# Attention with a sliding window, then a token-mixing MLP: queries kept in even and odd halves from the transposes to the output store

## The chip, the cores and the metric

One Trainium2 chip, one core of it. The metric is the device time of one execution in microseconds (us). Engines: TensorE (PE), VectorE (DVE), ScalarE (ACT), GpSimd (POOL) and SyncE (SP); here POOL issues all loads and SP all stores.

## What is computed

Eight batches, eight heads, 576 tokens, 64 features a head. Attention with a causal window of 128 tokens and a linear penalty on the distance, then an MLP that mixes tokens with weights made from the tokens themselves:

```python
scores = scale * np.matmul(q, k.transpose(0, 1, 3, 2))
rel = pos[:, None] - pos[None, :]
bias = slopes[:, None, None] * (-np.abs(rel).astype(np.float32))[None, :, :]
mask = (rel >= 0) & (rel < window)            # window = 128
scores = np.where(mask, scores + bias[None], -1000000000.0)
attn = softmax(scores)
x = np.matmul(attn, v)                        # heads side by side: (8, 576, 512)

wq, wk = x @ w_q, x @ w_k                     # (8, 576, 64) each
W_tok = scale * np.einsum('bsd,btd->bst', wq, wk)
mixed = np.einsum('bst,btd->bsd', W_tok, x)
out = np.maximum(mixed, 0.0) @ w_out          # (8, 576, 512), float32
```

## The kernel before

All work inside is fp16 with fp32 in PSUM. For each batch the kernel goes through these steps; the names in parentheses are the operations of its plan, with their lines.

- **Loads** (POOL, L239). Tokens 0 to 511 of q and k come in two chunks of 256 tokens into `nat`. In batches 1 to 5 a partition holds two neighbouring tokens of each head ("two-token rows": one transfer of 256 KB a chunk). In batches 6 and 7 (`ONE`) it holds one token ("one-token rows": two transfers of 128 KB a chunk). The last 64 tokens go to `ntl`, q below and k above. Batch 0 has a form of its own, six tokens a partition, in a part of the output buffer that is free at that time.
- **Transposes** (PE, L339 for batch 0, L366 for two-token rows, L360 for one-token rows, L382 for the tail) into a PSUM bank, 1024 columns a chunk, where tokens of even number stand ahead of those of odd number if the rows were two-token rows. An **eviction** (L220 on ACT, L222 on DVE, helper `cp`) copies the bank into `qkT`, which has the features on partitions and the tokens along the row, and puts even and odd tokens in turn as it does so.
- **Scores** (PE, L415): for each pair of heads and each half of the sequence, 64 keys at a time against their window of up to 192 queries, so that keys stand on the PSUM partitions and queries along the row. ACT takes the exponential (L420); DVE multiplies by the table of penalties `bt`, which is also the mask (L435, L439).
- **Values** (PE, L459) with a column of ones for the sum, DVE divides (L472, L475) into `x`, which has 128 tokens on partitions; PE transposes x (L491) and a copy puts it into `xT`.
- **Mixing** (PE, L508, L526, L538, L554; relu on ACT L561 or DVE L563), for two batches at a time up to the output: 1152 tokens in 9 tiles of 128. A tile is four matmuls (L575), a copy from PSUM into one of 14 output buffers `osa` (L220 on ACT or L222 on DVE), and a **store** by SP (L582) of 128 tokens x 512 float32, 256 KB. There are 36 tiles and 36 stores.

What runs when is fixed by a table, `ORDER`: every operation of the plan stands in it once, by its number, with a letter for its engine (A, D, G, S, P for ACT, DVE, POOL, SP, PE) and, for PE, its PSUM bank. Each engine works through its own operations in that order; between engines, semaphores guard data and buffers. A later tile that takes an output buffer again waits until the store of the earlier tile has landed. SP goes through its stores in the order of the table, which begins with tiles 12, 5, 3, 1, 13, 2, 0, 11.

At the start POOL writes the difference of column and row into `rel` (iota, L245), DVE makes the identity for the transposes from it (`idn`), and the table `bt` from the same numbers.

Of the kernel before, what the change touches and what calls it, by code (L numbers as in the profile page):

```python
# [13 lines left out]
P = 128  # L14
S = 576
# [16 lines left out]
175P5+1/4 141G 68D 20A 69D 89P0 176A 140G 24D 70P4 90D 152A 100P2 91D 227G 101D 188P0 102D 92P5 229G 189A  # L32
103P7 71A 230G 190D 155P0+1/2 93D 177P2 104D 231G 178A 191D 105P4+1/4 232G 156A 179D 240P7 416G 106A 180D
# [3 lines left out]
332P5 284A 339D 270P0 174A 233G 250P2 333D 251A 197P6 271A 234G 281P2 252D 330P5 198A 253D 414G 199A 200P4  # L37
272P0 201D 282A 327G 331D 259P6 336P4 273A 334P3 202P2 337A 610G 274D 203D 261P0+1/0 260A 335D 285D 353P2 262A
325G 340P4 275D 342P6 341A 129P1 286D 328G 354A 206P4 431P0 263D 329G 130A 264D 210P2 207A 418G 211A 287P4
326G 343A 254P2 288D 432A 289D 276P6 415G 425P1 255D 256D 290P0 419G 426A 204P4 277D 291D 265P2 602G 278D 205A  # L40
351P0 266D 352A 417G 257P5 344D 126P4 267D 506G 373P0 355D 127A 279P7 258D 507G 268P6 280D 123P5 269A 356D
424G 364P2 292P6 124D 365A 420G 345D 374A 362P4 423G 429P3 293D 363A 375P0 706G 294D 295P2 376A 427P5 510G
296A 430D 208P0 346P6 428A 377D 511G 366D 433P4 347D 209A 348D 435P2 297P5 434A 508G 457P0 298D 436A 303P4
458A 601G 304D 446P2+1/6 459P6 367D 357P0 460A 422G 448P4 447A 358D 461D 517P7 509G 359D 470P2 421G 378D 301P0
212P6 302A 518D 604G 449A 305P0 306A 608G 521P5+1/4 471A 437P0 349P7 603G 438A 523P4 350D 368P2 705G 213D 524A
379P0 701G 369D 450D 522A 468P6 380D 519P4 370D 609G 469A 525P5 439D 520A 605G 381D 371P7 120P6 526A 606G 472D
451D 382P4 527P0 614G 372A 299P2 440D 360P5 528A 221P7 607G 383D 361A 538P0 300D 697G 222A 384P4 121D 539A
704G 462D 616P7 385A 452P0 698G 617A 386D 560P2 215P6 516G 561A 453D 454D 562P4 514G 387P7 563A 473D 441P2
703G 620P1 216A 564D 529P4 618P0 611G 530A 565D 224P6 388A 512G 531D 540P4 619D 515G 307P7 541A 442D 716P0
513G 225A 542D 463P4 621A 443D 389P6 612G 308A 464D 622P1 717A 465D 613G 390A 551P2 623D 549P4 395P6 699G  # L50
712P0 550A 532D 624P1 396A 702G 713D 391P4 552A 474P6 625D 700G 392A 637P2 475D 626P0 476D 710G 720P5 627A
218P4 721D 638A 709G 628P0 543D 393P6 615G 397P2 629A 310P5 394A 708G 630D 533P0 219D 311A 650P6 711G 398A
534D 477P4 535D 444P5 651A 648P2 707G 553D 639P0 649A 445D 313P7 631D 640A 714P6 314D 718P5 715A 455P3 478D
566P0 554D 719A 316P2 567D 568D 735P4 317A 733P6 456D 632P0 736A 318S 641D 217S 131S 125S 724P2 734A 633D
555P4 634D 722P6 725A 556D 544P0 557D 723A 744P2 545D 399P5 546D 745A 659P6 726D 400A 746P0 642D 661P2 466P4
401S 662A 128S 122S 405P5 315S 223S 467D 660A 652D 643P2 747A 663D 479P6 644D 664D 406A 411P4 407S 480A 226S
312S 645D 558P5 481A 727D 569P1 482P0 412A 536P3 547P2 483D 559A 728P6 548D 537A 484P0 748D 570D 755P4 729D
485A 757P2 730D 408P1 756A 653D 758A 571P6 409A 749D 490P2 410S 665P0 309S 572A 214S 220S 413S 491D 646P5 573A
574P4 666D 654P2 667D 647A 635P7 575A 655D 488P0 492P5 656D 576P4 489A 636D 493A 657P3 737D 668P2 577A 486P0
658D 578P4 584P6 759D 503P3 579A 585D 487A 750P4 760D 669A 582P0 580P6 738D 402P2 583A 581A 751D 761P0 752D  # L60
504A 739P6 762D 763D 670P4 740D 731P3 741D 764P1 732A 753P0 765D 742P7 497P6 671D 743A 586P3 754A 403A 766P0
587D 589P7 588S 767A 673P3 672A 494P2 590D 768A 674D 769P5 592P7 498A 770D 499S 675P6 404S 591S 593A 771P3
495A 676D 496S 679P0 681P4 594S 772D 505S 683P6 595P2 680A 684D 682A 773P0 677P6 596A 775P4 598P3 678D 597S
776D 694P2 599A 691P7 695D 685P6 774D 696S 692D 500P5 686A 693S 777P0 687S 600S 779P2 501A 784P7 778D 502S
780D 688P6 785D 793P5 689D 786S 787P4 690S 794D 790P7 795S 788A 781P6 789S 791D 792S 782A 783S
"""
# [84 lines left out]

ONE = (6, 7)
PTW = 64 + 4 * 256
# [5 lines left out]
def kernel(  # L159
# [81 lines left out]
    def setup():  # L241
        plan.op("zero", ("DVE",), lambda e: nc.vector.memset(wz, 0.0), writes=["wz"])  # L242
        plan.op("one", ("DVE",), lambda e: nc.vector.memset(wone, 1.0), writes=["wone"])
        plan.op("iota", ("POOL",),
                lambda e: nc.gpsimd.iota(rel, pattern=[[1, 256]], base=0, channel_multiplier=-1),  # L245
                writes=["rel"])
        plan.op("idn", ("DVE",),
                lambda e: nc.vector.tensor_scalar(out=idn, in0=rel[:, 0:128], scalar1=0, scalar2=None,
                                                  op0=ALU.is_equal), reads=["rel"], writes=["idn"])
# [43 lines left out]
    def load_qk(b):  # L293
        if b == 0:
            for h in range(0, H, 2):
                for x, src in ((0, q), (1, k)):
                    load("ldsix", six[x][:, h : h + 2, :], src[b, h : h + 2].rearrange("h (p j) d -> p h (j d)", j=6),
                         [("six", x, h // 2)])
            return
        n = b % NN  # L300
        for c in range(2):
            for x, src in ((0, q), (1, k)):
                if b in ONE:
                    for j in range(2):
# [24 lines left out]
    def transposes(b):  # L329
        T = qkT[b % NQ]  # L330
        if b == 0:
            for hp in range(4):
                for x in range(2):
# [7 lines left out]

                    def ev(e, hp=hp, x=x, g=g):
                        cp(e, T[:, x, hp, :].rearrange("t (p j) -> t p j", j=6),
                           ps16(g)[:, 0:S].rearrange("t (j p) -> t p j", j=6))
# [5 lines left out]
        for z in range(2):  # L350
            for x in range(2):
                g = Ps(1)

                def tr(e, z=z, x=x, g=g):
                    o = ps16(g).rearrange("t (y j p) -> t y j p", y=4, j=2)
                    if b in ONE:
# [20 lines left out]
            if z == 0:  # L377
# [17 lines left out]
    def attention(b):  # L395
        for hp in range(4):
# [3 lines left out]
            for u in range(2):  # L400
                g = Ps(2)

                def sc(e, u=u, hp=hp, g=g):
# [7 lines left out]
                    for half, c, w, k0, q0 in mms:  # L411
                        for a in range(2):
                            r = slice(64 * a, 64 * a + 64)
                            o = 512 * a + c
                            nc.tensor.matmul(ps32(g)[half : half + 64, o : o + w],  # L415
                                             T[r, 1, hp, k0 : k0 + 64], T[r, 0, hp, q0 : q0 + w],
                                             start=True, stop=True)
# [81 lines left out]
    def mixing(b):  # L499
# [68 lines left out]
        for o in range(0, 512, 128) if i == 0 else range(512, 2 * S, 128):  # L568
# [12 lines left out]
            def st(e, o=o, n=n):  # L581
                nc.sync.dma_start(out=out[2 * p : 2 * p + 2].rearrange("b t c -> (b t) c")[o : o + 128, :], in_=osb[n])  # L582

# [54 lines left out]
```

## Time and profile before

| | |
|---|---|
| time, 3 runs | 150.2 us median (149.82 to 150.21) |
| profiled execution | 150.23 us, span 148.1 us |
| mean granted TensorE clock | 0.997 |
| loads (POOL's queue) | 14.82 MB in 85648 packets |
| stores (SP's queue) | 9.44 MB in 5184 packets, 36 transfers |
| first and last store issued | 101.9 and 144.9 us |

The span runs from the first instruction to the last; the profiled execution's own time is 2.1 us longer. In the rows, a group gives the line, the engine, the operation, output and input by the program's names, and "x" the number of instructions; three numbers with strokes are the shortest, the median and the longest duration in ns. The windows view gives, for a stretch of the span, the busy time of each engine. "A <- B" in the waits means that A waited and B released it. The DMA share in slices and windows is that of the 16 DMA engines; above 1 it counts packets that overlap.

### The profile page before, as it was taken

To read this page: it belongs to the slowest core of one execution; us is meant where nothing else is said; L and a number is where in the kernel's file an instruction comes from. 1 tells how busy PE (TensorE), PEld (TensorE's weight loads), DVE (VectorE), ACT (ScalarE), POOL (GpSimd) and SP (SyncE) were. 2 spreads that over 40 slices of the span, in tenths; PEclk is the share of its full clock that TensorE was granted. 3 is DMA by queue.
4 is the path that set the end of the run, shared out by engine and by line. 5 is a ranking of instruction groups with operands and counts; after the bars stand their busy time and mean duration, and the time that the engine had idled before them with its cause. 6 is when DMAs were issued, how large, how long until landed. Compare 5 with 4: busy or idle time off the path is not lost.

```text
span 148.1 us, 5381 instructions
## 1 busy us (share of the span) xinstructions
PE 136.3 (92%) x2314; PEld 88.3 (60%) x2314; DVE 119.0 (80%) x223; ACT 115.5 (78%) x181; POOL 85.6 (58%) x111
## 2 busy tenths in 40 slices
PE   6999889898799889999999999999999999999990
PEld 2345546676576476566576657576686858554430
DVE  1763799898979979988699989899989999367760
ACT  6428998789889988797999988998998984774311
POOL 6998999998565899599989996920000000000000
PEclk9999999999999999999999999999999999999998
DMA  2999999999999999999999999992586710158794
GB/s 20 147 145 163 169 162 123 157 177 175 181 174 182 168 146 148 180 156 149 157 156 156 151 136 148 106 134 93 222 302 252 293 61 4 71 189 304 265 341 180
DMA packets 90855, 24.59 MB, mean 166 GB/s; under 512 B 84176, under 2 KB 86224, under 8 KB 90832
## 3 DMA queue, kind: packets, MB, share of 16 engines
q0 software_dynamic: 85648, 14.82, 128.8%
q1 hardware_dynamic: 5184, 9.44, 17.1%
q8 instruction: 18, 0.29, 0.8%
q14 instruction: 5, 0.04, 0.1%
HBM read 29.62 MB, written 9.44 MB: 264 GB/s over the span
## 4 chain that ended last, share of the span: by engine, by line
PE 63%; ACT 17%; DVE 10%; issue 4%; POOL 2%; DMA 1%; DVEq 0%; POOLq 0%; ACTq 0%
PE psb L575 19%; PE psb L459 9%; ACT pt L420 8%; PE psb L415 7%; PE psb L491 6%; PE psb L508 5%; ACT qkT L220 4%; PE psb L554 4%; PE psb L366 3%; PE psb L360 3%; PE psb L538 3%; DVE x L475 2%; ACT rm L561 2%; PE psb L592 2%; PE psb L339 2%
## 5 line engine op out<-in xcount | busy, mean ns | idle before, releaser
L420 ACT ACTIVATE pt<-psb 128x768 f16<-128x768 f32 x64 | 49.8, 822 | 5.0 <-PE psb L415 3.5
L239 POOL DMA_DIRECT2D vn<-in_v_dram x44 | 36.7, 861 | 4.9 <-DMA natq<-in_q_dram 1.7
L575 PE MATMUL psb<-wout,rm 128*128 128x512 f16 x144 | 35.4, 380 | 0.3 <-ACT pt L420 0.3
L439 DVE TENSOR_TENSOR pt<-pt,bt 128x1536 f16<-128x1536 f16 x32 | 29.9, 950 | 0.2
L475 DVE TENSOR_TENSOR x<-psb,inv 128x640 f16<-128x640 f32 x32 | 26.1, 818 | 0.8
L220 ACT COPY qkT<-psb 128x1024 f16<-128x1024 f16 (+2 forms) x26 | 22.7, 891 | 4.3 <-PE psb L339 3.4
L415 PE MATMUL psb<-qkT 64*64 64x192 f16 (+2 forms) x640 | 21.1, 235 | 2.7 <-ACT qkT L220 1.3
L459 PE MATMUL psb<-vn,pt 128*128 128x65 f16 x576 | 22.3, 193 | 1.0 <-DVE pt L439 0.5
L459 PEld LDWEIGHTS <-pt 128*128 128x128 f16 x576 | 20.1, 98 | 4.0 <-DVE pt L439 0.7
L575 PEld LDWEIGHTS <-rm 128*128 128x128 f16 x144 | 12.6, 98 | 13.6 <-issue 1.7
L220 ACT COPY osa<-psb 128x512 f32<-128x512 f32 x23 | 13.6, 594 | 8.9 <-PE psb L575 7.7
L415 PEld LDWEIGHTS <-qkT 64*64 64x64 f16 x640 | 11.9, 106 | 12.5 <-issue 7.9
L222 DVE COPY qkT<-psb 128x1024 f16<-128x1024 f16 (+2 forms) x17 | 14.4, 856 | 5.2 <-PE psb L339 3.9
L239 POOL DMA_DIRECT2D natq<-in_q_dram x18 | 16.7, 936 | 0.7 <-DMA natk<-in_k_dram 0.4
L239 POOL DMA_DIRECT2D natk<-in_k_dram x18 | 16.8, 952 | 0.0
L435 DVE TENSOR_TENSOR pt<-pt,bt 128x512 f16<-128x512 f16 x32 | 13.2, 414 | 3.5 <-ACT pt L420 3.4
L592 PE MATMUL psb<-wz 128*128 128x512 f16 x38 | 14.2, 469 | 1.6 <-DVE wz L242 1.3
L561 ACT ACTIVATE rm<-psb 128x576 f16<-128x576 f32 x20 | 12.5, 663 | 2.3 <-PE psb L554 2.0
L491 PE MATMUL psb<-idn,x 128*128 128x128 f16 x160 | 12.7, 220 | 0.4 <-DVE x L475 0.2
L222 DVE COPY osa<-psb 128x512 f32<-128x512 f32 x13 | 8.8, 686 | 4.2 <-PE psb L575 2.9
L220 ACT COPY xT<-psb 128x576 f16<-128x576 f16 x15 | 9.4, 648 | 3.1 <-PE psb L491 3.1
L491 PEld LDWEIGHTS <-x 128*128 128x128 f16 x160 | 9.5, 98 | 2.6 <-DVE x L475 0.6
(63 smaller groups left out, 163.4 us busy)
## 6 DMA issues: line engine op xcount, KB each, us to landing
out_dram<-osa SPq DMA_DIRECT2D x36, 256.0 KB, 2.6
vn<-in_v_dram POOLq DMA_DIRECT2D x28, 128.0 KB, 5.2
natk<-in_k_dram POOLq DMA_DIRECT2D x10, 256.0 KB, 6.9
natq<-in_q_dram POOLq DMA_DIRECT2D x10, 256.0 KB, 6.8
vn<-in_v_dram POOLq DMA_DIRECT2D x16, 64.0 KB, 4.8
natq<-in_q_dram POOLq DMA_DIRECT2D x8, 128.0 KB, 5.3
natk<-in_k_dram POOLq DMA_DIRECT2D x8, 128.0 KB, 5.3
osa<-in_k_dram POOLq DMA_DIRECT2D x4, 144.0 KB, 4.6
```

Source lines behind the costliest of these rows:

```text
L220: nc.scalar.copy(o, i)
L222: nc.vector.tensor_copy(out=o, in_=i)
L239: plan.op(name, ("POOL",), lambda e: nc.gpsimd.dma_start(out=dst, in_=src), reads=reads, writes=writes)
L415: nc.tensor.matmul(ps32(g)[half : half + 64, o : o + w], T[r, 1, hp, k0 : k0 + 64], T[r, 0, hp, q0 : q0 + w], start=True, stop=True)
L420: nc.scalar.activation(out=blocks(pt)[:, :, 2 * u : 2 * u + 2, 0:192], in_=ps32(g).rearrange("t (a c) -> t a c", a=2)[:, :, 0:384].rearran ...
L439: nc.vector.tensor_tensor(out=o, in0=o, in1=bt[:, 2 * hp : 2 * hp + 2, 0:192].unsqueeze(2).broadcast_to([P, 2, 4, 192]), op=ALU.mult)
L459: nc.tensor.matmul(ps32(g)[:, o : o + D + 1], pt[:, a, c : c + 128], vv[:, kb, 2 * hp + a, 0 : D + 1], **flags)
L475: nc.vector.tensor_tensor(out=xb[:, :, 128 * hp : 128 * hp + 128].rearrange("t j (a d) -> t a j d", a=2), in0=px()[:, :, :, 0:D], in1=iv.u ...
L491: nc.tensor.transpose(ps16(g)[:, 128 * t : 128 * t + 128], xb[:, t, 128 * hp : 128 * hp + 128], idn)
L561: nc.scalar.activation(out=o, in_=s, func=AF.Relu, scale=WSCALE)
L575: nc.tensor.matmul(ps32(g), rm[p % NR][:, db, o : o + 128], wout[:, db, :], start=(db == 0), stop=(db == 3))
L592: nc.tensor.matmul(psb[:, b, :], wz[:, 0:P], wz[:, 0:DM], start=True, stop=True)
```

## The change

Queries are no longer put into the order of the tokens. For q, `qkT` now holds all even tokens and then all odd ones, as the transposes leave them in PSUM. From there on each strip of 64 queries (scores, weights, x, mixed tokens, output tile) has its 32 even tokens first and then its 32 odd ones; keys and values stay in order.

- The eviction of q copies 1024 columns as they lie (for batch 0, even and odd are parted on the way); that of the tail becomes two copies, one for q that parts even and odd, one for k.
- The moving operand of the scores takes, for each strip, 32 columns from the even half and 32 from the odd half.
- iota and the identity are written in the permuted order, so that penalties and transposes match.
- `ONE` holds batches 4 to 7, but for k alone: k of batches 4 and 5 now comes in one-token rows, q of batches 6 and 7 in two-token rows. The table is the same order with new numbers; where a load became two they stand side by side or near, where two became one the later is gone.
- A store of 128 tokens becomes two of 64 buffer rows, each with the even tokens and then the odd ones to their places in DRAM.

```diff
-ONE = (6, 7)
+ONE = (4, 5, 6, 7)
...
-                lambda e: nc.gpsimd.iota(rel, pattern=[[1, 256]], base=0, channel_multiplier=-1),
+                lambda e: nc.gpsimd.iota(rel, pattern=[[64, 4], [1, 2], [2, 32]], base=0, channel_multiplier=-1),
...
-                lambda e: nc.vector.tensor_scalar(out=idn, in0=rel[:, 0:128], scalar1=0, scalar2=None,
+                lambda e: nc.vector.tensor_scalar(out=idn.rearrange("t (s m j) -> t s m j", s=2, j=2),
+                                                  in0=rel[:, 0:128].rearrange("t (s j m) -> t s m j", s=2, j=2),
+                                                  scalar1=0, scalar2=None,
...
-                if b in ONE:
+                if x == 1 and b in ONE:
...
+                        if x == 0:
+                            cp(e, T[:, x, hp, :].rearrange("t (j p i) -> t j p i", j=2, i=3),
+                               ps16(g)[:, 0:S].rearrange("t (i j p) -> t j p i", i=3, j=2))
+                            return
                         cp(e, T[:, x, hp, :].rearrange("t (p j) -> t p j", j=6),
...
+                    if x == 0:
+                        cp(e, T[:, x].rearrange("t y (j p) -> t y j p", j=2)[:, :, :, P * z : P * z + P],
+                           ps16(g).rearrange("t (y j p) -> t y j p", y=4, j=2))
+                        return
...
-                    cp(e, T[:, :, :, 512:576], ps16(g)[:, 0:512].rearrange("t (y x c) -> t x y c", y=4, x=2))
+                    s = ps16(g)[:, 0:512].rearrange("t (y x c) -> t x y c", y=4, x=2)
+                    cp(e, T[:, 0].rearrange("t y (j p) -> t y j p", j=2)[:, :, :, 256:288],
+                       s[:, 0].rearrange("t y (p j) -> t y j p", j=2))
+                    cp(e, T[:, 1, :, 512:576], s[:, 1])
...
-                            nc.tensor.matmul(ps32(g)[half : half + 64, o : o + w],
-                                             T[r, 1, hp, k0 : k0 + 64], T[r, 0, hp, q0 : q0 + w],
+                            n = w // 64
+                            d = ps32(g)[half : half + 64, o : o + w].rearrange("t (s j m) -> t s j m", s=n, j=2)
+                            s = T[r, 0, hp, :].rearrange("t (j s m) -> t s j m", j=2, m=32)
+                            nc.tensor.matmul(d, T[r, 1, hp, k0 : k0 + 64], s[:, q0 // 64 : q0 // 64 + n],
...
-                nc.sync.dma_start(out=out[2 * p : 2 * p + 2].rearrange("b t c -> (b t) c")[o : o + 128, :], in_=osb[n])
+                d = out[2 * p : 2 * p + 2].rearrange("b t c -> (b t) c")
+                for z in range(2):
+                    nc.sync.dma_start(out=d[o + 64 * z : o + 64 * z + 64, :].rearrange("(m j) c -> j m c", j=2),
+                                      in_=osb[n][64 * z : 64 * z + 64])
```

The start of SP's list of stores, each with the semaphores that it waits for (DMAHW0 to 7 are eight counters that the transfers of SP take in turn, and each transfer waits for the one that last had its counter; DMASW are those of the loads). Before:

```order
L582 DMA out_0_dram<-osa_112 128x512 [waits DMASW0_49,Activation_49]
L582 DMA out_0_dram<-osa_112 128x512 x2
L582 DMA out_0_dram<-osa_112 128x512 [waits DVE_49]
L582 DMA out_0_dram<-osa_112 128x512 [waits DMASW5_49,Activation_49]
L582 DMA out_0_dram<-osa_112 128x512
```

In the changed kernel:

```order
L601 DMA out_0_dram<-osa_112 2x32x512 [waits DMASW0_49,Activation_49]
L601 DMA out_0_dram<-osa_112 2x32x512 x5
L601 DMA out_0_dram<-osa_112 2x32x512 [waits DVE_49]
L601 DMA out_0_dram<-osa_112 2x32x512
L601 DMA out_0_dram<-osa_112 2x32x512 [waits DMAHW0_49,DMASW5_49,Activation_49]
L601 DMA out_0_dram<-osa_112 2x32x512 [waits DMAHW1_49]
```

Each store stands there twice, its DRAM side has even/odd as its first dimension, and the first wait for a counter of SP's own comes with the fifth tile instead of the ninth.

On ACT, the evictions of batch 1 (`qkT1`) between the exponentials of batch 0 (`pt`), before:

```order
L220 COPY qkT1_83<-psb_113 128x4x256
L420 ACTIVATE pt3_89<-psb_113 128x2x2x192
L220 COPY qkT1_83<-psb_113 128x4x256
L420 ACTIVATE pt2_88<-psb_113 128x2x2x192
L220 COPY qkT1_83<-psb_113 128x8x64
```

And in the changed kernel:

```order
L222 COPY qkT1_83<-psb_113 128x4x256
L437 ACTIVATE pt3_89<-psb_113 128x2x2x192
L222 COPY qkT1_83<-psb_113 128x8x128
L437 ACTIVATE pt2_88<-psb_113 128x2x2x192
L222 COPY qkT1_83<-psb_113 128x8x32
L222 COPY qkT1_83<-psb_113 128x4x64
```

Nothing moved there; q's copy (the second) has another shape, and the tail's copy has become two.

More of the change, by code (lines that the diff above doesn't have):

```diff
@@ L32 @@
 175P5+1/4 141G 68D 20A 69D 89P0 176A 140G 24D 70P4 90D 152A 100P2 91D 227G 101D 188P0 102D 92P5 229G 189A
-103P7 71A 230G 190D 155P0+1/2 93D 177P2 104D 231G 178A 191D 105P4+1/4 232G 156A 179D 240P7 416G 106A 180D
+103P7 71A 230G 190D 155P0+1/2 93D 177P2 104D 231G 178A 191D 105P4+1/4 232G 156A 179D 240P7 417G 418G 106A 180D
 166P0 108P6 322G 157D 109A 158D 181P2 107A 320G 110P6 167A 182D 192P4 241A 319G 168D 238P1 193D 183D 111A 239A
@@ L36 @@
 247D 27G 118P4 243A 172D 196A 248P6 119D 283P2 235G 249A 114P0 115D 162P5 184P4 163A 173P7 338P6 236G 185A
[L37 to L65, printed above, removed]
+332P5 284A 339D 270P0 174A 233G 250P2 333D 251A 197P6 271A 234G 281P2 252D 330P5 198A 253D 414G 415G 199A
@@ new lines @@
+200P4 272P0 201D 282A 327G 331D 259P6 336P4 273A 334P3 202P2 337A 612G 274D 203D 261P0+1/0 260A 335D 285D
+353P2 262A 325G 340P4 275D 342P6 341A 129P1 286D 328G 354A 206P4 433P0 263D 329G 130A 264D 210P2 207A 420G
+211A 287P4 326G 343A 254P2 288D 434A 289D 276P6 416G 427P1 255D 256D 290P0 421G 428A 204P4 277D 291D 265P2
+606G 278D 205A 351P0 266D 352A 419G 257P5 344D 126P4 267D 508G 509G 373P0 355D 127A 279P7 258D 510G 268P6 280D
+123P5 269A 356D 426G 364P2 292P6 124D 365A 422G 345D 374A 362P4 425G 431P3 293D 363A 375P0 706G 294D 295P2
@@ new lines @@
+376A 429P5 514G 296A 432D 208P0 346P6 430A 377D 515G 366D 435P4 347D 209A 348D 437P2 297P5 436A 511G 512G
+459P0 298D 438A 303P4 460A 605G 304D 448P2+1/6 461P6 367D 357P0 462A 424G 450P4 449A 358D 463D 521P7 513G 359D
+472P2 423G 378D 301P0 212P6 302A 522D 608G 451A 305P0 306A 525P5+1/4 473A 439P0 349P7 607G 440A 527P4 350D
+368P2 705G 213D 528A 379P0 703G 369D 452D 526A 470P6 380D 523P4 370D 611G 471A 529P5 441D 524A 609G 381D 371P7
+120P6 530A 610G 474D 453D 382P4 531P0 616G 372A 299P2 442D 360P5 532A 221P7 383D 361A 542P0 300D 699G 222A
@@ new lines @@
+384P4 121D 543A 464D 618P7 385A 454P0 700G 619A 386D 564P2 215P6 520G 565A 455D 456D 566P4 518G 387P7 567A
+475D 443P2 622P1 216A 568D 533P4 620P0 613G 534A 569D 224P6 388A 516G 535D 544P4 621D 519G 307P7 545A 444D
+716P0 517G 225A 546D 465P4 623A 445D 389P6 614G 308A 466D 624P1 717A 467D 615G 390A 555P2 625D 553P4 395P6
+701G 712P0 554A 536D 626P1 396A 704G 713D 391P4 556A 476P6 627D 702G 392A 639P2 477D 628P0 478D 710G 720P5
+629A 218P4 721D 640A 709G 630P0 547D 393P6 617G 397P2 631A 310P5 394A 708G 632D 537P0 219D 311A 652P6 711G
@@ new lines @@
+398A 538D 479P4 539D 446P5 653A 650P2 707G 557D 641P0 651A 447D 313P7 633D 642A 714P6 314D 718P5 715A 457P3
+480D 570P0 558D 719A 316P2 571D 572D 735P4 317A 733P6 458D 634P0 736A 318S 643D 217S 131S 125S 724P2 734A 635D
+559P4 636D 722P6 725A 560D 548P0 561D 723A 744P2 549D 399P5 550D 745A 661P6 726D 400A 746P0 644D 663P2 468P4
+401S 664A 128S 122S 405P5 315S 223S 469D 662A 654D 645P2 747A 665D 481P6 646D 666D 406A 411P4 407S 482A 226S
+312S 647D 562P5 483A 727D 573P1 484P0 412A 540P3 551P2 485D 563A 728P6 552D 541A 486P0 748D 574D 755P4 729D
@@ new lines @@
+487A 757P2 730D 408P1 756A 655D 758A 575P6 409A 749D 492P2 410S 667P0 309S 576A 214S 220S 413S 493D 648P5 577A
+578P4 668D 656P2 669D 649A 637P7 579A 657D 490P0 494P5 658D 580P4 491A 638D 495A 659P3 737D 670P2 581A 488P0
+660D 582P4 588P6 759D 505P3 583A 589D 489A 750P4 760D 671A 586P0 584P6 738D 402P2 587A 585A 751D 761P0 752D
+506A 739P6 762D 763D 672P4 740D 731P3 741D 764P1 732A 753P0 765D 742P7 499P6 673D 743A 590P3 754A 403A 766P0
+591D 593P7 592S 767A 675P3 674A 496P2 594D 768A 676D 769P5 596P7 500A 770D 501S 677P6 404S 595S 597A 771P3
@@ L66 @@
+497A 678D 498S 681P0 683P4 598S 772D 507S 685P6 599P2 682A 686D 684A 773P0 679P6 600A 775P4 602P3 680D 601S
+776D 696P2 603A 693P7 697D 687P6 774D 698S 694D 502P5 688A 695S 777P0 689S 604S 779P2 503A 784P7 778D 504S
+780D 690P6 785D 793P5 691D 786S 787P4 692S 794D 790P7 795S 788A 781P6 789S 791D 792S 782A 783S
 """
@@ L355, in tr @@
                     o = ps16(g).rearrange("t (y j p) -> t y j p", y=4, j=2)
-                    if b in ONE:
+                    if x == 1 and b in ONE:
                         w = nat[x][n][:, z].rearrange("p (j e) -> p j e", j=2)
```

## Prediction

> **What bounds the kernel now.** I read the page from the top: busy shares, the span in 40 slices, then the chain that ended last.
>
> ```profile
> span 148.1 us, 5381 instructions
> ...
> PE 136.3 (92%) x2314; PEld 88.3 (60%) x2314; DVE 119.0 (80%) x223; ACT 115.5 (78%) x181; POOL 85.6 (58%) x111
> ...
> PE   6999889898799889999999999999999999999990
> ...
> DMA  2999999999999999999999999992586710158794
> GB/s 20 147 145 163 169 162 123 157 177 175 181 174 182 168 146 148 180 156 149 157 156 156 151 136 148 106 134 93 222 302 252 293 61 4 71 189 304 265 341 180
> ...
> PE 63%; ACT 17%; DVE 10%; issue 4%; POOL 2%; DMA 1%; DVEq 0%; POOLq 0%; ACTq 0%
> ```
>
> TensorE is busy 92% of the span and 63% of the chain; the chain holds 1% of DMA. The slices show two kinds of traffic: the loads up to about slice 27 (100 us), at about 150 GB/s, and after them the stores in bursts, with slices of 4 and 61 GB/s between. So stores cost nothing today except where a buffer comes free late. Next, two stretches and two bursts in the windows view (its last three columns are granted clock, mean busy share of the DMA engines, GB/s):
>
> ```profile
> core 0: us, PE busy (x) PEld busy (x) DVE busy (x) ACT busy (x) POOL busy (x), PEclk, DMA share, GB/s
> 10.00:71.00 61.00, 54.82 (x1163) 37.83 (x1161) 51.23 (x98) 53.13 (x80) 52.44 (x67) 1.00 1.96 163
> 71.00:148.00 77.00, 72.91 (x1098) 47.06 (x1096) 62.41 (x112) 58.40 (x93) 24.25 (x29) 0.99 1.16 178
> 103.30:105.30 2.00, 2.00 (x45) 1.32 (x42) 1.93 (x5) 1.82 (x3) 0.00 (x0) 1.00 1.01 381
> 117.30:118.90 1.60, 1.60 (x26) 1.23 (x26) 1.60 (x5) 1.45 (x3) 0.00 (x0) 1.00 1.03 384
> ```
>
> TensorE idles about 6 us between 10 and 71 us and about 4 us afterwards; any gain of ACT or DVE can only shrink these. In the two bursts all 16 DMA engines are full (share 1.01 and 1.03) and move 381 to 384 GB/s: **24 GB/s for one engine** that carries stores. Third, the stores themselves, in the queue part, the issue part, the view of the output tile and SP's waits:
>
> ```profile
> q1 hardware_dynamic: 5184, 9.44, 17.1%
> ...
> out_dram<-osa SPq DMA_DIRECT2D x36, 256.0 KB, 2.6
> ```
> ```profile
> L582 SPq DMA_DIRECT2D out_dram<-osa x36: 332/402/1405, 101.9 to 144.9; - x36
> ...
> DMA to landing us min/median/max: 2.0/2.6/4.8
> ```
> ```profile
> SPq L582 <- ACT osa L220: 97.9, 7, 88.7
> ```
>
> The first store is issued at 101.9 us although tiles are ready earlier: SP's list begins with tile 12 and waits 88.7 us for it. All 9.44 MB then leave in the last 45 us. And 5184 packets in 36 stores are 144 each: 128 rows of 2 KB, and 16 packets more, one for each of 16 engines.
>
> **The change: the stores.** By the rows of SP in the section on the change, 36 transfers of 128x512 become 72 of 2x32x512: each half takes 64 partitions and writes its even tokens and then its odd ones, so on the DRAM side the leading dimension is 2 (even or odd) and the 32 tokens come second. Nothing in this trace has so small a leading dimension: stores lead with 128, loads with 128, 96 or 64, all multiples of 16, and the 16 extra packets of each store say that 16 engines shared it, 8 rows each. How a transfer with a leading 2 is shared out is therefore the unknown on which everything hangs. Lower end: it is still spread over 16 engines, and data cost what they cost now. Upper end: it is cut along its leading dimension and goes to two engines, the even half on one and the odd half on the other. The row to which I hold is 144 = 128 + 16: pieces are dealt whole along the leading dimension, and a dimension of 2 has only two pieces. I take **two engines**.
>
> The Trainium skill, page "DMA: Bandwidth & Descriptors", section "Why a DMA increments its semaphore by 16 and not by 1", states that the hardware looks at the outermost dimension that is not 1 on both sides of a copy and uses the largest number of engines, up to 16, that divides both; from the SP queue these are the lowest-numbered ones. By that rule each half (64 on the one side, 2 on the other) runs on engines 0 and 1, and so do all 72; the 16 extra packets of each store today agree with it, and no run so far shows a 2.
>
> Price: two engines at 24 GB/s are 48 GB/s, and 9.44 MB take 9.44/0.048 = **197 us**. Other routes to it: q1's share of 17.1% is 0.171 x 16 x 148.1 = 405 us of engine time, over two engines 203 us; a tile (256 KB) takes 5.5 us in place of 0.69 us. Is the stream ever without work? A tile costs TensorE about 1 us (four of the 144 matmuls of L575, whose 35.4 us are in a row below), and at 101.9 us most of the 14 output buffers are full already. Later tiles wait for a buffer, thus for a store, and each is refilled within a few us while up to a dozen other tiles stand in line at 5.5 us each. So from 101.9 us on the stores set the pace; TensorE, ACT and DVE stand waiting for buffers, and what they do costs nothing more. The end of the kernel now:
>
> ```profile
> 141.66 0.70 DVE osa L222
> 142.37 0.02 issue
> 142.38 1.89 DMA out_dram<-osa
> 144.27 0.57 ACT osa L220
> ```
>
> Here already a copy (144.27) waits for a store to free its buffer. Last issue 144.9 us, soonest landing 2.0 us later, at 146.9, so 1.2 us lie between the last landing and the end of the span. An issue takes 2.0 us to land, of which 0.69 us is data at 381 GB/s, so 1.3 us is latency. Sum: 101.9 + 1.3 + 197 + 1.2 = **301.4 us of span**. The profiled execution took 150.23 us with a span of 148.1, so 2.1 us lie around it, and its time stands 0.03 us from the median of 150.2: 301.4 + 2.1 = 303.5, say **303 us**.
>
> By the same page's section "Where 436 GB/s comes from", an engine's ceiling is 436/16 = 27.2 GB/s; with it the data would take 173 us and the sum be 280 us, an estimate of the best case.
>
> **The other edits** count only as far as they move 101.9 us, and their cover is that stream; uncovered prices follow.
>
> ```profile
> L415 PE MATMUL psb<-qkT 64*64 64x192 f16 (+2 forms) x640 | 21.1, 235 | 2.7 <-ACT qkT L220 1.3
> ...
> L575 PE MATMUL psb<-wout,rm 128*128 128x512 f16 x144 | 35.4, 380 | 0.3 <-ACT pt L420 0.3
> ```
> ```profile
> L220 ACT COPY qkT<-psb x26: 586/1012/1131, 10.4 to 100.1; 128x1024 f16<-128x1024 f16 x17, 128x512 f16<-128x512 f16 x5, 128x576 f16<-128x576 f16 x4
> ```
> ```profile
> L222 DVE COPY qkT<-psb x17: 414/756/1225, 7.6 to 93.3; 128x1024 f16<-128x1024 f16 x11, 128x576 f16<-128x576 f16 x4, 128x512 f16<-128x512 f16 x2
> ...
>   PE psb L415: 0.2, 1
>   PE psb L508: 0.2, 1
> ```
> ```profile
> 21.14 0.71 ACT pt L420
> 21.85 0.49 ACT qkT L220
> ```
> ```profile
> L239 POOL DMA_DIRECT2D natk<-in_k_dram x18: 883/952/1017, 7.6 to 89.8; - x18
> ```
> ```profile
> L245 POOL IOTA rel<- x1: 394/394/394, 3.4 to 3.4; 128x256 int32 x1
> ```
>
> Last, all that TensorE waited for from 45 us to the end (us in total, times, longest):
>
> ```profile
> PE psb L459 <- ACT rm L561: 0.4, 1, 0.4
> PE psb L575 <- ACT pt L420: 0.3, 1, 0.3
> PE psb L554 <- DVE gm L222: 0.3, 1, 0.3
> PE psb L592 <- ACT pt L420: 0.2, 1, 0.2
> ```
> ```profile
> L222 DVE COPY qkT<-psb x1: 692/692/692, 93.3 to 93.3; 128x1024 f16<-128x1024 f16 x1
> ```
>
> - q's eviction without interleaving: three of DVE's copies of 1024 (at 20.7, 46.8 and 70.7 us) are now strided q copies at about 1215 ns and would go at about 690 ns, as the one at 93.3 us does: 3 x 0.53 = 1.6 us of DVE. On ACT both kinds take about 1012 ns, so nothing. TensorE waited only 0.2 + 0.2 us for DVE's copies, so at most 0.4 us of it can show.
> - The tail copy in two: ACT takes 586 ns for 512 elements and 1012 for 1024, so 0.16 us fixed and 0.83 ns an element; 256 elements are 0.37 us, twice that 0.75, 0.16 more, on five copies; on DVE (414 and 692) 0.14 more, on two. One of them, at 21.85 us, is in the chain: +0.2 us.
> - The scores read q in runs of 32 elements. 640 matmuls hold 21.1 us; lower end nothing, upper end a doubling, +21 us. The nearest row is their own: 235 ns on average for up to 192 columns, well above the streaming, which leaves room; I take nothing.
> - The loads: two-token k loads of batches 4 and 5 become eight short ones, and short q loads of 6 and 7 become four long ones; count and bytes stay. In between POOL runs one issue late, two at most, at 0.95 us each. These loads land after 45 us, and none of TensorE's waits from there on ends with a load, so some of it is covered: 0 to +1.9 us, I take 0. Sixteen transposes of 64 columns against eight of 128 swap places between k and q: 0.
> - iota and the identity in strided form at the start: 0 to a doubling of iota, +0.4 us; I take 0.1.
>
> Together +0.3 us before 101.9 us, inside the rounding of 303.
>
> **The rivals.** (1) *Still sixteen engines.* For it: the SBUF side leads with 64, a multiple of 16, and if the hardware deals by that side nothing changes in the data. Then the price is the uncovered one: the last tile's second half is issued one issue (0.33 us, plus a gap) after the first, +0.4; the tail copy +0.2; the start +0.1: 150.2 + 0.7 = 150.9, say **151 us**. (2) *Not slower*, the other side: the same sixteen engines, and DVE's shorter q copies reach TensorE in the stretch from 10 to 71 us, where it idles 6 us. DVE gains 1.6 - 0.3 = 1.3 us there; it decides against the 0.7 us above, so if more than 0.7 of the 1.3 us is passed on, the kernel comes out at 150.2 or below, at best 150.2 + 0.7 - 1.3 = **149.6 us**. Against it: only 0.4 us of TensorE's waits end with a DVE copy. (3) *Two engines that also get in each other's way.* One half's two engines read partitions p and p+32 at the same moment; should these share one path with the speed of one engine, data take 9.44/0.024 = 393 us and the time is **500 us**; a partial clash lies between. Against it: at 8 rows an engine, today's sixteen have pairs that lie 32 partitions apart too, and are full at 24 GB/s each.
>
> The Trainium skill, page "SBUF — State Buffer", describes a port layout (its terms: port swizzle) in which partitions 32 apart share a DMA port; by that rule the third rival would happen whenever the two engines keep step, and the 381 GB/s of the bursts speak against a lasting step.
>
> **How the numbers follow.** Two engines 0.76; sixteen engines 0.17 (of which slower by over 0.3%, about what a measurement of this kernel can tell from no change, 0.10; within 0.3% 0.05; faster 0.02); clash 0.07, spread evenly from 303 to 500. The forecast is 303 us. Its own range: up to 315 by the 203 us of engine time, the scores' first few us and a late start; down to 278 if two engines, alone on a path that sixteen fill, are an eighth quicker (an allowance; no row shows it). Two engines alone hold less than 8 in 10, so the range reaches into the clash, to 400: 0.76 + 0.04 = 0.80. Slower 0.76 + 0.07 + 0.10 = 0.93.
>
> **What would show it.** With two engines: q1's packets become 36 x 128 + 72 x 2 = 4752 (with sixteen, 36 x 128 + 72 x 16 = 5760); DMA share after 102 us stands at 2/16 = 0.12 with 48 GB/s, flat to the end; copies to osa and TensorE wait for stores; TensorE's share falls to about 45%; the first store is still issued at 102 us, give or take 1. DVE's q copies show 690 ns and the tail copies 0.37 on ACT. The prediction is wrong if the windows after 102 us show 300 GB/s or more; if one engine proves much quicker alone than 24 GB/s; or if the stream has holes because a buffer comes too late.

## The result and the profile after

The changed kernel takes **294.18 us** (median of 4 runs, 294.14 to 294.81) against 150.2 us: the ratio is 1.959, with a 95% interval of 1.953 to 1.965. The profiled execution took 294.81 us with a span of 293.0 us; it is the slowest of the four by 0.6 us.

The page of the changed kernel, the lines that answer to those of before:

```profile
span 293.0 us, 5436 instructions
...
PE 147.6 (50%) x2314; PEld 93.5 (32%) x2314; DVE 118.4 (40%) x225; ACT 116.5 (40%) x186; POOL 85.4 (29%) x111
...
PE   8988989998999991046938304960004000000000
...
PEclk9999999999999999558797755895555555555555
DMA  7999999999999911111111111111111111111111
GB/s 86 158 161 129 167 177 176 154 148 157 160 160 131 94 27 51 51 51 53 51 53 51 51 51 51 53 51 51 51 51 51 51 51 51 52 51 51 51 51 39
...
q1 hardware_dynamic: 4752, 9.44, 8.4%
```

A slice is 7.3 us here, so the first 14 are the first 102 us, and they look like those of before. From slice 16 on the DMA rows are flat: 51 to 53 GB/s, one tenth busy, up to the last one. The engines do their work in pieces between long holes. And the stores are 4752 packets in place of 5184: 36 x 128 rows as before, and 144 more, which is two for each of 72 transfers. The windows view of the long stretch, with the first and the last us of the data:

```profile
core 0: us, PE busy (x) PEld busy (x) DVE busy (x) ACT busy (x) POOL busy (x), PEclk, DMA share, GB/s
150.00:200.00 50.00, 23.39 (x134) 11.86 (x134) 9.70 (x16) 9.89 (x17) 0.00 (x0) 0.74 0.13 51
250.00:290.00 40.00, 0.00 (x0) 0.00 (x0) 0.69 (x1) 0.00 (x0) 0.00 (x0) 0.50 0.13 51
103.50:104.25 0.75, 0.75 (x28) 0.58 (x25) 0.62 (x3) 0.75 (x2) 0.00 (x0) 1.00 0.00 0
104.25:104.50 0.25, 0.25 (x14) 0.25 (x11) 0.25 (x1) 0.13 (x1) 0.00 (x0) 1.00 0.15 33
104.50:105.50 1.00, 1.00 (x36) 0.83 (x32) 0.97 (x3) 0.69 (x1) 0.00 (x0) 1.00 0.11 12
105.50:106.50 1.00, 0.99 (x19) 0.59 (x16) 0.96 (x3) 1.00 (x3) 0.00 (x0) 1.00 0.12 41
...
291.50:291.80 0.30, 0.00 (x0) 0.00 (x0) 0.00 (x0) 0.00 (x0) 0.00 (x0) 0.50 0.05 20
291.80:293.00 1.20, 0.00 (x0) 0.00 (x0) 0.00 (x0) 0.00 (x0) 0.00 (x0) 0.50 0.00 0
```

A share of 0.13 is two of sixteen engines (0.125), so each carries 25.5 GB/s; which two they are the profile does not tell. The data begin at about 104.3 us and end at 291.8. The stores as instructions, and who waits for them (the view of the output tile, then the waits of all engines: us in total, times, longest):

```profile
L601 SPq DMA_DIRECT2D out_dram<-osa x72: 513/2442/4500, 103.0 to 278.6; - x72
```
```profile
DVE osa L224 <- DMA out_dram<-osa: 61.0, 4, 30.1
...
ACT osa L222 <- DMA out_dram<-osa: 42.7, 5, 18.0
PE psb L592 <- DVE osa L224: 39.3, 2, 26.3
```

The first store is issued at 103.0 us. An issue lasts 2.4 us at the median, about the 2.6 us that its 128 KB take at 51 GB/s, so SP goes at the pace of the data. The copies into the output buffers wait 104 us for stores; TensorE then waits for those copies.

### The profile page after: what moved, and what is told of

The parts are those of the page before. It is cut to its first block, busy times and chain, and to the rows that moved or that the text cites. A ratio compares the mean times of both kernels' runs of the same rounds, so it can differ in the third digit from the quotient of the medians.

```text
span 293.0 us, 5436 instructions
## 1 busy us (share of the span) xinstructions
PE 147.6 (50%) x2314; PEld 93.5 (32%) x2314; DVE 118.4 (40%) x225; ACT 116.5 (40%) x186; POOL 85.4 (29%) x111
## 3 DMA queue, kind: packets, MB, share of 16 engines
q1 hardware_dynamic: 4752, 9.44, 8.4%
HBM read 29.62 MB, written 9.44 MB: 133 GB/s over the span
## 4 chain that ended last, share of the span: by engine, by line
DMA 40%; SPq 16%; POOL 15%; PE 12%; issue 2%; DVE 2%; ACT 2%; POOLq 0%; ACTq 0%; DVEq 0%
DMA out_dram<-osa 28%; SPq L601 16%; POOL vn L241 6%; DMA natq<-in_q_dram 5%; PE psb L592 4%; DMA wout<-in_moe_w_out_dram 4%; POOL natk L241 2%; DMA natk<-in_k_dram 2%; POOL natq L241 2%; PE psb L508 2%; POOL ntl L241 2%; PE psb L476 2%; POOL osa L241 2%; PE psb L433 1%; ACT osa L222 1%
## 5 line engine op out<-in xcount | busy, mean ns | idle before, releaser
L592 PE MATMUL psb<-wout,rm 128*128 128x512 f16 x144 | 39.5, 411 | 39.6 <-DVE osa L224 39.3
L592 PEld LDWEIGHTS <-rm 128*128 128x128 f16 x144 | 13.5, 103 | 55.2 <-issue 44.5
L508 PE MATMUL psb<-idn,x 128*128 128x128 f16 x160 | 15.4, 249 | 22.8 <-ACT osa L222 22.4
L476 PE MATMUL psb<-vn,pt 128*128 128x65 f16 x576 | 23.0, 195 | 3.8 <-ACT osa L222 2.5
L241 POOL DMA_DIRECT2D natk<-in_k_dram x22 | 20.1, 937 | 0.6 <-issue 0.3
L508 PEld LDWEIGHTS <-x 128*128 128x128 f16 x160 | 11.8, 112 | 25.5 <-issue 22.9
L224 DVE COPY qkT<-psb 128x1024 f16<-128x1024 f16 (+2 forms) x19 | 13.2, 711 | 5.3 <-PE psb L343 3.9
L241 POOL DMA_DIRECT2D natq<-in_q_dram x14 | 13.0, 938 | 1.1 <-DMA natq<-in_q_dram 0.7
L224 DVE COPY xT<-psb 128x576 f16<-128x576 f16 x17 | 7.6, 453 | 9.1 <-PE psb L508 9.1
```

What stands on the lines that cost most here:

```text
L224: nc.vector.tensor_copy(out=o, in_=i)
L241: plan.op(name, ("POOL",), lambda e: nc.gpsimd.dma_start(out=dst, in_=src), reads=reads, writes=writes)
L476: nc.tensor.matmul(ps32(g)[:, o : o + D + 1], pt[:, a, c : c + 128], vv[:, kb, 2 * hp + a, 0 : D + 1], **flags)
L508: nc.tensor.transpose(ps16(g)[:, 128 * t : 128 * t + 128], xb[:, t, 128 * hp : 128 * hp + 128], idn)
L592: nc.tensor.matmul(ps32(g), rm[p % NR][:, db, o : o + 128], wout[:, db, :], start=(db == 0), stop=(db == 3))
```

## The experiments

Each edit is one of the changed kernel, if not said otherwise. In the runs that change only the stores, the program is the same up to the first store, which SP issues between 102.3 and 103.6 us.

**1. Whole stores: all of the change but its stores.**

```diff
-                d = out[2 * p : 2 * p + 2].rearrange("b t c -> (b t) c")
-                for z in range(2):
-                    nc.sync.dma_start(out=d[o + 64 * z : o + 64 * z + 64, :].rearrange("(m j) c -> j m c", j=2),
-                                      in_=osb[n][64 * z : 64 * z + 64])
+                nc.sync.dma_start(out=out[2 * p : 2 * p + 2].rearrange("b t c -> (b t) c")[o : o + 128, :], in_=osb[n])
```

> The changed kernel, but with one store of 128 rows a tile as before, so that the rows of each strip reach DRAM with the even tokens first (the only part of the computation that differs). Theory (two engines, because the DRAM side of a store leads with a dimension of 2): all but some 1 us of the loss is gone, 150 to 152 us, q1 packets 5184, bursts of 380 GB/s. Rival (the rest of the change, that is the scores' split reads, the loads or the waits, has a good part in the loss): 160 us or more.

150.96 us, ratio 1.0056 (1.0026 to 1.0086), 5184 packets. All of the loss but 0.7 us is in the stores, and those 0.7 us are a loss too.

**2. The converse: the kernel before with nothing but the new stores.**

> The kernel before with nothing but the change's stores (72 of 2x32x512); the rows of each strip reach DRAM parted wrongly. Theory (the stores carry the whole loss): 293.5 us, that is the changed kernel's 294.2 less the 0.7 us that the other edits cost in the run with whole stores; q1 packets 4752. Rival (the stores are dear only together with the other edits): well below 290 us.

293.73 us, ratio 1.953 (1.942 to 1.965), 4752 packets. The stores carry the loss by themselves, and the two parts add up (293.7 + 0.7 against 294.2 us).

**3. Other leading dimensions: 4 and 8 on 64 partitions, 2 and 16 on 128.** The diffs show j=4 and j=2; those with 8 and 16 differ in that number alone.

```diff
-                    nc.sync.dma_start(out=d[o + 64 * z : o + 64 * z + 64, :].rearrange("(m j) c -> j m c", j=2),
+                    nc.sync.dma_start(out=d[o + 64 * z : o + 64 * z + 64, :].rearrange("(m j) c -> j m c", j=4),
```
```diff
-                for z in range(2):
...
+                nc.sync.dma_start(out=d[o : o + 128, :].rearrange("(m j) c -> j m c", j=2), in_=osb[n])
```

> As the change, but each half is cut into 4 x 16 rows on the DRAM side and not into 2 x 32; rows reach DRAM in another order than the reference's. Theory: four engines at 25.5 GB/s, 9.44 MB in 93 us after about 105 us, so 200 us (195 to 206); q1 packets 36 x 128 + 72 x 4 = 4896; DMA share 0.25. Rival (rows that are apart in DRAM are slow to write, whatever the number of engines): about 294 us as before. Rival (the hardware deals by the 64 partitions and the loss is elsewhere): 294 us.

> As the change, but 8 x 8 rows on the DRAM side; rows reach DRAM in another order than the reference's. Theory: eight engines, 204 GB/s, 9.44 MB in 46 us against the 45 us in which the kernel before sends its stores, so the stores only just fall behind: 153 us (150 to 158), q1 packets 36 x 128 + 72 x 8 = 5184. Rivals as for the run with four: about 294 us.

> The changed kernel with one store a tile, all 128 partitions, cut into 2 x 64 rows on the DRAM side; rows reach DRAM in another order. Theory (the leading dimension of 2 alone decides): two engines, 36 x 128 + 36 x 2 = 4680 packets, 51 GB/s, 294 us. Rival (two engines that read partitions p and p+32 hinder each other; here they are p and p+64): 54 GB/s or more, 283 us or less. Rival (the 72 halves or their 64 partitions cost): near 150 us.

> The changed kernel with one store of 128 partitions a tile, cut into 16 x 8 rows on the DRAM side, so that neighbouring partitions write rows 16 apart; rows reach DRAM in another order than the reference's. Theory (only the size of the leading dimension counts): sixteen engines, bursts of 380 GB/s, 151 us like whole stores in order (150.96). Rival (rows that lie apart in DRAM cost, and with 2, 4 and 8 this grew as the number of engines fell): 155 us or more.

| leading dimension, partitions | packets of the stores | engine time, us | time, us | ratio (interval) |
|---|---|---|---|---|
| 2, 64 (the change) | 4752 = 4608 + 72 x 2 | 394 | 294.18 | 1.959 (1.953 to 1.965) |
| 2, 128 | 4680 = 4608 + 36 x 2 | 389 | 294.07 | 1.956 (1.944 to 1.967) |
| 4, 64 | 4896 = 4608 + 72 x 4 | 396 | 201.76 | 1.340 (1.335 to 1.346) |
| 8, 64 | 5184 = 4608 + 72 x 8 | 447 | 165.03 | 1.097 (1.093 to 1.101) |
| 16, 128 | 5184 = 4608 + 36 x 16 | 488 | 152.37 | 1.012 (1.008 to 1.016) |
| 128, 128 (whole stores) | 5184 = 4608 + 36 x 16 | 405 | 150.96 | 1.006 (1.003 to 1.009) |

The engine time is what the packets of the stores took on all engines together: the queue's share of 16 engines, times 16, times the span. The shares of the last two rows:

```profile
q1 hardware_dynamic: 5184, 9.44, 20.3%
...
q1 hardware_dynamic: 5184, 9.44, 17.0%
```

Windows of the run with four, two of that with eight, and one of that with sixteen:

```profile
150.00:190.00 40.00, 11.75 (x50) 4.59 (x48) 7.47 (x11) 3.16 (x6) 0.00 (x0) 0.68 0.26 102
```
```profile
110.00:120.00 10.00, 8.68 (x153) 6.46 (x153) 8.39 (x16) 8.22 (x15) 0.00 (x0) 1.00 0.53 177
128.00:129.00 1.00, 1.00 (x6) 0.41 (x5) 0.18 (x1) 1.00 (x3) 0.00 (x0) 1.00 0.53 199
```
```profile
104.00:106.00 2.00, 2.00 (x45) 1.32 (x42) 1.93 (x5) 1.83 (x3) 0.00 (x0) 1.00 1.00 330
```

The last two columns are the reading. With four, 0.26 of the engines move 102 GB/s, which is 25.5 for one engine, as with two. With eight, 0.53 (all eight full) move 177 GB/s, and 199 in the best microsecond. In every run with 2, 4, 8 or 16 the extra packets of a transfer are its leading dimension, and the more engines, the shorter the time. The run with 2 on 128 partitions excludes the number of transfers and the halves as causes: 36 transfers are as slow as 72.

Two expectations missed. Eight engines were expected at 153 us, since 46 us of data, at 204 GB/s, against a stretch of 45 us seemed to fit. But the stores took 447 us of engine time there and not 394, which is 56 us for each of eight: the engines were full most of the time from the first issue, at 102.3 us, to the last, at 158.4, and copies into the buffers waited 11.6 us for stores. And sixteen engines with rows 16 apart were expected at 151: they took 152.4, against 151.0 for whole stores in order (in another set of runs, and the intervals of the ratios just overlap). Here too the engine time says that it is more: 488 us against 405, and full engines move 330 GB/s where the kernel before shows 381 to 384. So the way in which rows are dealt out costs something with eight and with sixteen engines, and nothing with two and four. The rival put it down to rows that lie apart in DRAM; but which partitions are read at the same time may change with the leading dimension as well, and no run tells the two apart.

**4. Halves with a leading dimension of 64.** In these runs a store is two transfers that spread over sixteen engines.

```diff
-                    nc.sync.dma_start(out=d[o + 64 * z : o + 64 * z + 64, :].rearrange("(m j) c -> j m c", j=2),
+                    nc.sync.dma_start(out=d[o + 64 * z : o + 64 * z + 64, :],
```

> The changed kernel with two stores a tile as in the change, but each to 64 neighbouring rows (leading dimension 64 on both sides); the rows of each strip reach DRAM with the even tokens first. Theory (leading dimension of 2): sixteen engines again, 151 to 152 us, q1 packets 36 x 128 + 72 x 16 = 5760. Rival (72 transfers of 64 partitions are themselves slow: they read half the partitions, take twice the issues, and use up SP's eight counters twice as fast): 200 us or more.

160.94 us, ratio 1.070 (1.066 to 1.074): sixteen engines by the 5760 packets, and yet 10 us more than whole stores. The theory of the leading dimension stands, but halves cost something else. Two runs to find it: halves by columns, and halves by even and odd partitions.

```diff
+                    nc.sync.dma_start(out=d[o : o + 128, 256 * z : 256 * z + 256], in_=osb[n][:, 256 * z : 256 * z + 256])
...
+                    nc.sync.dma_start(out=d[o : o + 128, :].rearrange("(m j) c -> j m c", j=2)[z],
+                                      in_=osa[z : 128 : 2, n])
```

> The changed kernel with two stores a tile, each of all 128 partitions and half the columns (128x256, 1 KB rows); the rows of each strip reach DRAM with the even tokens first. It tells apart why two stores of 64 partitions with neighbouring rows took 160.9 us where 151 to 152 were expected. Theory A (64 partitions use half of the ways out of SBUF, so 16 engines are held at 200 GB/s): here the bursts go above 250 GB/s and the time is 151 to 154 us. Theory B (SP needs 0.6 us to issue each of 72 transfers, 128 KB each, so 210 GB/s is what issues allow): about 161 us here too.

> The changed kernel with two stores a tile of 64 partitions each as in the run with 64 neighbouring rows (160.9 us), but the first takes the even partitions of the buffer and the second the odd ones, each to every second row of the tile; the rows of each strip reach DRAM with the even tokens first. Theory A (64 neighbouring partitions use half of the ways out of SBUF; even ones use all): bursts above 250 GB/s, SP's issues at about 0.45 us, 151 to 154 us. Theory B (a transfer of 64 rows is slow by its issue, 0.6 us each): 161 us again.

Columns: 154.61 us, 1.029 (1.024 to 1.034), bursts of 277 GB/s. That spoke for theory A. Even and odd partitions: **161.46 us**, 1.073 (1.066 to 1.079), and that is theory B. SP's stores, the queue and one window of each of the three; first 64 neighbouring partitions:

```profile
q1 hardware_dynamic: 5760, 9.44, 25.6%
```
```profile
L601 SPq DMA_DIRECT2D out_dram<-osa x72: 466/596/1747, 102.3 to 156.2; - x72
```
```profile
111.50:113.50 2.00, 2.00 (x47) 1.95 (x48) 1.21 (x4) 1.95 (x4) 0.00 (x0) 1.00 0.88 209
```

Then even and odd partitions:

```profile
q1 hardware_dynamic: 5760, 9.44, 16.0%
```
```profile
L601 SPq DMA_DIRECT2D out_dram<-osa x72: 472/594/2173, 102.3 to 156.0; - x72
```
```profile
111.50:113.50 2.00, 1.69 (x39) 1.68 (x39) 0.80 (x3) 1.95 (x5) 0.00 (x0) 1.00 0.55 204
```

And half the columns:

```profile
L601 SPq DMA_DIRECT2D out_dram<-osa x72: 332/441/1670, 102.3 to 149.4; - x72
```

Theory A is right about the packets and wrong about the time. With neighbouring partitions the engines are busy 0.256 x 16 x 159.5 = 653 us in all, with even and odd ones 0.160 x 16 x 159.0 = 407 us: rows of 64 neighbours take 1.6 times as long to move. But both kernels run at 204 to 209 GB/s, and with even and odd partitions the engines are half idle (0.55). What sets both is SP, whose issues follow one another there with hardly a gap (even and odd partitions):

```profile
109.68 5.71 SPq L601 DMA_DIRECT2D out_dram<-osa  x9
```

Nine issues of 128 KB in 5.71 us are 207 GB/s. With 128 partitions an issue takes 0.441 us at the median, which would allow 297, and the bursts reached 277. Why an issue of 64 rows takes longer than one of 128 (466 against 332 ns at the least) no run shows.

**5. The 0.7 us of the other edits: the loads and transposes as before.** From the run with whole stores, with the table of the kernel before:

```diff
-ONE = (4, 5, 6, 7)
+ONE = (6, 7)
...
-                if x == 1 and b in ONE:
+                if b in ONE:
```

> The changed kernel with whole stores, and with the loads, the table and the transposes of q and k as before (one-token rows for q and k of batches 6 and 7 alone); queries of batches 6 and 7 enter in another order, and the rows of each strip reach DRAM with the even tokens first. Theory (of the 0.7 us that the kernel with whole stores lost, most is the swap of transposes: 16 of 64 columns take about 0.1 us more of TensorE than 8 of 128, which shows in batches 6 and 7, where TensorE never waits, and not in 4 and 5, where it does): 150.3 to 150.5 us. Rival (the split tail copy, the start and the scores' split reads cost the 0.7 us): 151.0 us.

150.47 us, ratio 1.0008 (0.998 to 1.004): no longer to be told from before. The intervals of the two runs overlap slightly, so the traces must say the rest. Against the kernel before, the exponential that starts there at 98.19 us starts 0.20 us later with the new loads and 0.07 with the old ones; that at 103.47 us 0.70 and 0.34. Loads, table and transposes change together in this run; by the timelines, most of the difference fits the transposes. TensorE's timeline, before:

```profile
98.96 0.61 PE L360 MATMUL psb<-idn,natq 128*128 128x128 f16 x8
99.41 0.44 PE L491 MATMUL psb<-idn,x 128*128 128x128 f16 x5
```

and in the run with whole stores:

```profile
99.25 0.64 PE L374 MATMUL psb<-idn,natq 128*64 128x128 f16 x16
99.83 0.45 PE L508 MATMUL psb<-idn,x 128*128 128x128 f16 x5
```

From the first start to that of the next group it is 0.45 us for eight and 0.58 for sixteen. q of batches 6 and 7 has four such groups, where TensorE is busy throughout: about 0.5 us by this one. The swap the other way, for k of batches 4 and 5, takes about 0.1 us off: the exponential at 70.88 us starts 0.02 us earlier with the new loads and 0.07 later with the old ones. The 0.07 us that remain from 23 us on are the tail's copy. A step of 0.27 us, common to both runs, begins at a reciprocal of DVE (at 100.61 us before), for which DVE idles 0.18 us with the old loads and not at all in the kernel before; what it waits for the traces leave open.

**6. A version that computes all of the reference without the new stores.** From whole stores: the mixing matmuls (L571) put q back into order, with stretches of 320 and 256 queries, either in reading (the diff) or in writing.

```diff
-                        nc.tensor.matmul(ps32(g)[:, 512 * a : 512 * a + 288], gm[m][r, 128 * j : 128 * j + 128],
-                                         (wq2 if a else wT)[m][r, 288 * c : 288 * c + 288], start=True, stop=True)
+                        nc.tensor.matmul(ps32(g)[:, 512 * a : 512 * a + w].rearrange("t (s m j) -> t s m j", j=2, m=32), gm[m][r, 128 * j : 128 * j + 128],
+                                         (wq2 if a else wT)[m][r, c0 : c0 + w].rearrange("t (s j m) -> t s m j", j=2, m=32), start=True, stop=True)
```

> The changed kernel with q's tokens put back into order in the last step before the output: the mixing matmuls read their moving operand token by token, 64 bytes apart, in stretches of 320 and 256 queries in place of 288, and whole stores of 128 rows follow as in the kernel before. Computes all of the reference. Theory (a moving operand is read at full speed whatever its step, as the scores' runs of 32 showed): 64 matmuls as long as before, 151.0 us, the time with whole stores. Rival (single columns 64 bytes apart are read at a fraction of the speed): the 64 matmuls of 0.29 us double or quadruple, +9 to +28 us on a TensorE that never waits from 80 us on, 155 to 175 us.

> As the kernel that reads the mixing operand token by token, but the operand is read as it lies and the result written to PSUM in steps of two columns. Computes all of the reference. Theory: as fast, 151.0 us. Rival (PSUM takes columns two apart more slowly): 155 us or more.

Reading in steps: 154.81 us, 1.028 (1.024 to 1.032). Writing in steps: 153.89 us, 1.022 (1.018 to 1.027). Both theories fell; both times lie just under the ranges of the rivals. The matmuls of whole stores, then of reading in steps:

```profile
L571 PE MATMUL psb<-wT,gm x32: 279/293/293, 35.3 to 139.4; 64*128 64x288 f16 x32
```
```profile
L571 PE MATMUL psb<-wT,gm x32: 400/436/473, 35.3 to 143.1; 64*128 64x256 f16 x16, 64*128 64x320 f16 x16
```

A matmul grows from 0.293 to 0.436 us for the same 288 columns on average. The 64 matmuls run in pairs, each on half of the partitions, at the same time (whole stores):

```profile
139.22 0.29 PE L571 MATMUL psb<-wT,gm 64*128 64x288 f16 x1
139.22 0.29 PE L571 MATMUL psb<-wq,gm 64*128 64x288 f16 x1
```

So they cost 32 x 0.143 = 4.6 us (TensorE's busy time rises from 136.3 to 141.1), and 3.9 us of that reach the end. With steps in writing the medians are 422 and 428 ns. So neither repairs the change: no version here beats the kernel before.

## Why the prediction was right, step by step

**The engines of a store.** Right, as reasoned: 4752 packets, two for each transfer, and the runs with 2, 4, 8 and 16 show the cause by itself. The rule of the Trainium skill (page "DMA: Bandwidth & Descriptors", section "Why a DMA increments its semaphore by 16 and not by 1"), that the outermost dimensions of the two sides set the number of engines, agrees with all rows of the table.

**The rate.** 24 GB/s for an engine was taken from bursts in which all sixteen were full; two alone make 25.5, so the data take 9.44/0.051 = 185 us and not 197. That is the term that was off. The lower end of the range held a little for it, as an allowance that no row showed. The Trainium skill, page "DMA: Bandwidth & Descriptors", section "Where 436 GB/s comes from", gives what sixteen ports carry; the 27.2 GB/s for an engine that the prediction worked out from it, an estimate, were not reached in the windows above.

**The start and the end.** The first store was issued at 103.0 us, 1.1 us later than taken over from before; this is the slowest of the four executions, and with whole stores SP began at 102.3. Its first data moved 1.3 us later and the last ones ended 1.2 us before the end of the span, both as forecast. From the first data to the last it is 187.5 us, since the stream started slowly (12 GB/s in the window from 104.5). The sum is 103.0 + 1.3 + 187.5 + 1.2 = 293 us of span, where 301.4 was forecast.

**No hole in the stream.** Right: DMA stays at 51 to 53 GB/s in every slice from the 16th until the last. TensorE's share came out at 50% and not 45%, because its busy time rose from 136 to 148 us at a granted clock of 0.50 to 0.74 (a matmul of the output tiles took 411 ns on average in place of 380).

**The other edits**, seen in the run with whole stores: +0.3 us expected, +0.7 measured. Right in size were DVE's q copies (the first line), and nearly so the tail's copies; the lines are of the changed kernel:

```profile
46.92 0.68 DVE L224 COPY qkT<-psb 128x1024 f16<-128x1024 f16 x1
...
49.11 0.61 DVE L224 COPY qkT<-psb 128x256 f16<-128x256 f16 x2
```
```profile
21.71 0.70 ACT L222 COPY qkT<-psb 128x256 f16<-128x256 f16 x2
```

The first took 1.22 us before. The pair on ACT takes 0.70 us against 0.63 before, so +0.07 and not +0.2; the pair on DVE 0.61 against 0.41. The scores' split reads cost nothing (236 ns on average against 235). Wrong was the step "Sixteen transposes of 64 columns against eight of 128 swap places between k and q: 0": most of what k gains lies where TensorE waits anyway, what q loses where it never does.

**The rivals.** Sixteen engines would hardly have given 151 us. The run with halves of 64 rows shows what I left out there: SP's issues of 64 rows take 0.6 us and not 0.33, and that kernel came to 161 us. The rival on the other side, 149.6 us, was out of reach for the same reason, and whole stores, with DVE's shorter copies, took 151.0 and not less than before. The clash of two engines that read partitions 32 apart did not occur: 51 GB/s with partitions p and p+32, and 51 with p and p+64 (partitions by the order of the rows; the profile does not show them). That today's sixteen engines have such pairs too, which the prediction held against this rival, no run shows. The page "SBUF — State Buffer" of the Trainium skill, whose port layout lay behind that rival, shows itself elsewhere: rows of 64 neighbouring partitions, by its layout on half the ports, took 1.6 times as long with all sixteen engines at work.

## What to carry to other kernels

Look at the outermost dimension of both sides of a transfer before anything else: here 2 in place of 128 took the stores from 381 GB/s to 51, and the extra packets of a queue divided by its transfers tell how many engines share one. A change that saves little on the engines (here 1.2 us of DVE's 119, with whole stores) must not move its disorder to the output; to undo it in a matmul's access cost 3 to 4 us as well. What a swap between two stages is worth depends on which of them has idle time on the bounding engine.

## What the runs showed of the hardware that was not expected

An issue by SP takes between 332 and 591 ns at the least by the shape of the transfer: 332 for 128x512 and 128x256, 466 for 64x512, 513 for 2x32x512, 538 for 16x8x512, 591 for 8x8x512. The same 9.44 MB cost between 389 and 488 us of engine time by the way their rows are dealt out, and 653 from 64 neighbouring partitions on sixteen engines. And the granted TensorE clock goes down to 0.50 where TensorE waits for long (the PEclk row above), and recovers only in the busier slices.
